# Turning keys and queries in fp32, in place and two head pairs at a time, with the instruction order drawn anew

## The chip, the cores and the metric

The kernel runs on one core of one Trainium2 chip. The metric is device time in microseconds (us): the median of several executions. The profile shows one further execution, taken by the hardware profiler. The engines are called as in the profile: PE is TensorE, DVE is VectorE, ACT is ScalarE, POOL is GpSimd, SP is SyncE, whose queue issues most of the DMAs.

## What is computed

Attention over selected chunks, and then a gated feed-forward layer. Cut from the reference:

```python
# q, k, v: 4 x 8 x 768 x 64 float32; chunks of 32 keys, 24 chunks; top_k = 6
k_min = np.min(k_chunks, axis=3); k_max = np.max(k_chunks, axis=3)
ub = sum(maximum(q * k_min, q * k_max), axis=-1)     # bound of each query on each chunk
ub = where(causal, ub, -1e9)
top_chunks = argsort(ub, axis=-1)[..., -6:]
scores = q @ k.T / 8
scores = where(selected and causal, scores, -1e9)
attn = softmax(scores)
x = (attn @ v), heads side by side                   # 3072 x 512
out = (sigmoid(x @ w_gate) * (x @ w_val)) @ w_out    # w_gate, w_val 512 x 1536; w_out 1536 x 512
```

## The kernel before

**Units.** The 3072 tokens are eight units, u0 to u7, of 384 tokens each. A unit goes through attention (bounds, choice, scores, exponential, mask, product with v) and then through the feed-forward layer. u0 to u2 hold the early tokens and turn their keys and queries on PE. Units u3 to u7 hold the later query blocks of batches 1 to 3 and turn keys and queries with DVE's 32 x 32 transposes; the change is about these.

**Keys of a batch** (`keys_blocks`, steps k, k16, kt, kx, hk, kcr). Four DMAs on SP (`load_blocks`, L660) bring the 768 keys of eight heads so that 32 x 32 blocks can be turned. For each of the four head pairs: the smallest and largest of every chunk straight from the raw fp32 tile by a DVE reduction that transposes as it reads (`extremes`, L684); a copy to f16 on POOL or ACT (k16, L459, L455); a DVE transpose of that copy (kt, L850); and two copies of it into the tiles that the scores read (hk, one for each head of the pair).

**Queries** (`turn_queries`, `queries_blocks`, `choose`). A DVE transpose per head pair takes the raw fp32 tile into a second tile qf (L866). From qf come the positive part qm (L698, L700) and the f16 copies hq. PE multiplies qf and qm with the chunk ranges in fp32 (ub, L899), the even and the odd heads each into a PSUM tile of their own. DVE transposes each (ubn, L910), bars unseen chunks (ubm), finds the largest eight of each row (mx, MAX8, L922), compares with the sixth (ap, L927) and transposes the result (apt, L933), again once for each of the two. Copies hqm put this mask beside the queries, so that the scores' matmul adds it.

**Attention's end** (`finish`). DVE divides by the row sums (rz L1012, x L1014). For u3 to u7 a transposing DMA on SP (L1019, step xT) turns x for the feed-forward layer.

**Feed-forward.** For u3 to u7 gate and value products (L1199) are made with seven products of half size in the place of eight: they need sums of weights (ss, L1170) and of tokens (tt, L1183), and steps that put the products together (e7, sd, c21, c22). The output projections of u4 to u7 are made in the same manner: sums of output weights (tw, L1052, twelve of them) and of hidden blocks (sw, L1082), products at L1092. The others are plain (o, L1321). DVE or POOL makes the sums.

**Order and room.** Every step is an operation with a cost per engine; a written list, ORDER, gives their sequence and each one's engine in 2097 entries (`kt_3_2=V` is the turning of batch 3's head pair 2 on DVE; P is PE, A ACT, V DVE, G POOL, S SP). Every engine, and SP's queue, works through its own part in that sequence. A second list, SLOTS, gives each buffer its place in one SBUF arena of 234 units, and each PSUM tile one of eight banks; a buffer may be written when the earlier holders of its place were last read. A third list, TIES, adds a few waits. Names end in unit or batch and part: x_u3_1 is x of unit 3, head pair 1.

Of the kernel before, what the change touches and what calls it, by code (L numbers as in the profile page):

```python
# [14 lines left out]
NEG = -60000.0  # L15
UNITS = 234
# [123 lines left out]
tanh_u1_6=A cm_u2_2=G v_u1_2=P hg_u1_9=V k11_2=S kcr_1=G osb_u0_2=A exp_u2_2_1=A sc_u2_1_2=P exp_u2_0_2=A exp_u2_3_1=A sc_u2_7_1=P  # L140
qf0_u3_1=V k10_2=S sc_u2_6_2=P pv_u2_4=P hq0_u3_0=G exp_u2_6_2=A hg_u1_7=V qf0_u3_2=V pv_u2_5=P v_u1_10=P v_u1_8=P exp_u2_7_1=A qf0_u3_3=V
qm_u3_0=A cm_u2_6=G exp_u2_1_2=A hg_u1_3=V v_u1_6=P hq1_u3_0=G hg_u1_2=V v_u1_11=P hg_u1_6=V hq1_u3_2=G hg_u1_11=V qm_u3_2=A ub_u3=P
hg_u1_8=V k01_2=S xpsf_3_0=P hq0_u3_2=G hk0_1_3=A ss3_g0=G o0_u1_1=P pv_u2_0=P ubn1_u3=V hk1_1_3=A ubn0_u3=V ubm1_u3=V xpsf_3_1=P
xTf_3_1=A kt_1_1=V mx1_u3=V hk1_1_2=A pv_u2_3=P hk0_1_1=A pv_u2_6=P xTf_3_0=A q00_2=S hg_u1_10=V qf0_u4_0=V pv_u2_2=P o1_u1_1=P v16_1_1=G
pv_u2_1=P pv_u2_7=P hk1_1_1=G ap1_u3=V rz_u2_2=V rz_u2_3=V apt1_u3=V rz_u2_0=V hk0_1_0=G x_u2_3=V rz_u2_1=V ubm0_u3=V o2_u1_1=P o0_u1_0=P
x_u2_2=V hk0_1_2=A o1_u1_0=P x_u2_0=V hqm1_u3_2=A q11_2=S osb_u1_1=A xps_u2_3=P sc_u3_7_1=P xT_u2_3=A exp_u3_7_1=A sc_u3_7_2=P mx0_u3=V
qf0_u4_2=V x_u2_1=V hqm1_u3_0=G sc_u3_4_0=P ap0_u3=V exp_u3_4_0=A v16_1_2=G kx1_2_1=V k16_2_3=G xps_u2_2=P apt0_u3=V xT_u2_2=A kx1_2_2=V
sc_u3_5_0=P exp_u3_7_2=A k16_2_0=G hqm0_u3_2=G q01_2=S o0_u1_2=P sc_u3_6_2=P sc_u3_4_2=P exp_u3_4_2=A sc_u3_6_1=P qf0_u4_1=V qf0_u4_3=V
exp_u3_5_0=A o1_u1_2=P k16_2_2=G exp_u3_6_2=A kx0_2_0=V hqm0_u3_0=G sc_u3_5_2=P kt_2_0=V exp_u3_5_2=A exp_u3_6_1=A xps_u2_1=P q10_2=S
sc_u3_6_0=P cm_u3_5=G sc_u3_4_1=P kt_2_3=V exp_u3_6_0=A cm_u3_6=G sc_u3_7_0=P xps_u2_0=P out_u0_1=S o2_u1_0=P xT_u2_1=A kx0_2_2=V  # L150
o2_u1_2=P kx1_2_3=V v_1_3=S xT_u2_0=A g_u2_2=P sc_u3_1_2=P v_1_4=S exp_u3_4_1=A sc_u3_0_1=P g_u2_11=P exp_u3_7_0=A cm_u3_4=G v_1_0=S
cm_u3_7=G sc_u3_5_1=P osb_u1_2=A exp_u3_1_2=A osb_u1_0=A kx0_2_3=V sc_u3_1_0=P k16_2_1=G hk0_2_3=G tanh_u2_11=A v_u2_0=P v_2_1=S
exp_u3_1_0=A cm_u3_1=G exp_u3_0_1=A exp_u3_5_1=A sc_u3_3_1=P qf1_u4_3=V sc_u3_1_1=P exp_u3_1_1=A exp_u3_3_1=A tanh_u2_2=A g_u2_8=P
hk1_2_0=G out_u1_0=S g_u2_10=P qf1_u4_2=V out_u1_1=S kx1_2_0=V qf1_u4_0=V k01_3=S k11_3=S sc_u3_0_2=P v_u2_10=P qf1_u4_1=V sc_u3_3_2=P
g_u2_9=P tanh_u2_10=A hq1_u4_2=G hg_u2_10=V kx0_2_1=V hq0_u4_2=G exp_u3_0_2=A tanh_u2_8=A g_u2_4=P sc_u3_2_1=P v_u2_8=P qf0_u5_1=V
qm_u4_2=A v16_1_3=G v_u2_9=P sc_u3_3_0=P exp_u3_3_2=A hq1_u4_0=G hg_u2_8=V kcr_2=G tanh_u2_9=A out_u0_2=S hg_u2_9=V sc_u3_0_0=P g_u2_0=P
exp_u3_2_1=A qm_u4_0=A g_u2_5=P v16_1_4=G exp_u3_0_0=A qf0_u5_2=V v16_1_0=G ub_u4=P cm_u3_0=G g_u2_3=P exp_u3_3_0=A hk1_2_3=G qf0_u5_3=V
pv_u3_6=P qf0_u5_0=V tanh_u2_0=A k10_3=S tanh_u2_4=A kt_2_1=V sc_u3_2_0=P v16_2_1=G qm_u5_0=A v_u2_11=P ubn0_u4=V tanh_u2_5=A qm_u5_2=A
ubn1_u4=V exp_u3_2_0=A hq1_u5_0=A hk0_2_1=G g_u2_7=P tanh_u2_3=A ubm0_u4=V out_u1_2=S pv_u3_0=P sc_u3_2_2=P exp_u3_2_2=A hg_u2_0=V
mx0_u4=V kt_2_2=V hq1_u5_2=A pv_u3_4=P pv_u3_1=P ap0_u4=V ubm1_u4=V tanh_u2_7=A hg_u2_11=V pv_u3_7=P apt0_u4=V g_u2_1=P v_1_5=S hq0_u4_0=G  # L160
hk1_2_1=G pv_u3_5=P g_u2_6=P tanh_u2_1=A mx1_u4=V k00_3=S hqm0_u4_2=A rz_u3_3=V v_u2_7=P cm_u3_3=G ub_u5=P hg_u2_7=V ap1_u4=V hk0_2_0=G
hk0_2_2=G tanh_u2_6=A x_u3_3=V sc_u4_2_0=P ubn1_u5=V sc_u4_2_2=P apt1_u4=V hqm0_u4_0=A v_u2_4=P v_u2_5=P rz_u3_2=V exp_u4_2_2=A
sc_u4_2_1=P rz_u3_0=V exp_u4_2_0=A sc_u4_1_1=P exp_u4_2_1=A hk1_2_2=G cm_u3_2=G v_u2_1=P hqm1_u4_2=G v_2_0=S ubn0_u5=V hqm1_u4_0=G
# [12 lines left out]
exp_u4_0_3=A pv_u4_0=P v_2_2=S sc_u5_5_0=P p6_g1_u3=P osb_u2_2=A sd_g0_u3=A p6_g0_u3=P p2_g0_u3=P sc_u4_5_2=P tanh_u3_100=A exp_u5_5_0=A
tanh_u3_000=A pv_u4_1=P x_u4_1=V cm_u4_5=G exp_u4_5_2=A p7_g2_u3=P e7_g2_u3=A p1_g2_u3=P tt3_u3=G c21_g1_u3=V p5_g1_u3=P c21_g0_u3=V
# [223 lines left out]
def kernel(  # L401
# [1065 lines left out]
```

## Time and profile before

| | |
|---|---|
| median of 3 runs | 274.91 us (274.8 to 275.87) |
| the profiled execution | 274.87 us |
| its span in the trace | 273.0 us |
| granted TensorE clock, mean | 0.994 |
| PE busy | 263.1 us, 3094 matmuls |
| DVE, ACT, POOL busy | 227.3, 208.6, 187.3 us |

The span runs from the first to the last instruction in the trace; 274.87 also holds what lies around it. Busy time is the time in which an engine executes something. PEld is PE's weight load, which lies beside its matmuls. In a row of a group stand the line, engine, operation, output and input, their shapes and the count, then the busy time of all and the mean ns of one, and last the idle time ahead of them with what ended it. A row of one line's instructions has the shortest, the median and the longest duration. A timeline row has start, duration, engine, line and operation, and in brackets the idle time before it and what ended that.

### The profile page before, as it was taken

The page shows a single profiled execution, that of the slowest core. Times are in us where ns is not written, and L with a number is a line of the kernel's source. Part 1 is how long each engine was busy: PE and PEld are TensorE (multiplying, and loading weights), DVE is VectorE, ACT ScalarE, POOL GpSimd, SP SyncE. Part 2 cuts the span into 40 slices and gives each one's busy share as a digit, 9 for nine tenths or more (in the row PEclk, how much of TensorE's full clock was granted, in tenths as well). Part 3 has the DMA queues.
Part 4 walks back from the last instruction along what each step waited for, and adds up shares of the span by engine and source line. Part 5 has one row for each costly group of instructions (what it writes and reads, how often), then busy time and mean ns, then how long its engine had stood idle before and what let it go on. Part 6 is the DMA issues. An engine that isn't in the chain of part 4 may idle for free.

```text
span 273.0 us, 8339 instructions
## 1 busy us (share of the span) xinstructions
PE 263.1 (96%) x3094; PEld 207.8 (76%) x3094; DVE 227.3 (83%) x654; ACT 208.6 (76%) x451; POOL 187.3 (69%) x287
## 2 busy tenths in 40 slices
PE   6979999999999999999999999999999999999994
PEld 4655658657666667675889878899988999999984
DVE  4789846788989989889989999889898879678861
ACT  6378878669886899899889999989998763665322
POOL 5796744658996799697499974887773556584440
PEclk9979999999999999999999999999999999999999
DMA  6999999999999999912783715130200020022035
GB/s 155 240 292 200 204 214 214 214 184 177 170 204 165 202 257 218 180 33 53 166 133 86 195 31 130 42 95 4 46 14 2 17 46 1 2 78 79 2 119 228
DMA packets 131576, 34.74 MB, mean 127 GB/s; under 512 B 119760, under 2 KB 128464, under 8 KB 131536
## 3 DMA queue, kind: packets, MB, share of 16 engines
q1 hardware_dynamic: 126768, 29.50, 50.8%
q0 software_dynamic: 4768, 4.72, 10.2%
q8 instruction: 24, 0.39, 0.6%
q14 instruction: 16, 0.13, 0.1%
HBM read 30.67 MB, written 6.29 MB: 135 GB/s over the span
## 4 chain that ended last, share of the span: by engine, by line
PE 85%; DVE 4%; DMA 4%; ACT 2%; issue 1%; POOL 1%; SPq 1%; DVEq 0%; ACTq 0%
PE sc_u L960 11%; PE g_u L1247 9%; PE o_u L1321 9%; PE v_u L1247 8%; PE pl_v_u L1199 7%; PE pv_u L993 6%; PE pl_g_u L1199 6%; PE pl_u L1092 6%; PE ps_v_u L1199 5%; PE ps_g_u L1199 4%; PE ps_u L1092 4%; PE ube_u L899 3%; DMA arena<-arena 3%; ACT arena L971 1%; DMA arena<-in_k_dram 1%
## 5 line engine op out<-in xcount | busy, mean ns | idle before, releaser
L971 ACT ACTIVATE arena<-sc_u 128x512 f16<-128x512 f32 (+3 forms) x184 | 90.4, 552 | 7.7 <-PE sc_u L960 6.3
L1082 POOL TENSOR_TENSOR arena<-arena 128x256 f16<-128x256 f16 x44 | 29.1, 682 | 23.6 <-DVE arena L1082 9.7
L977 POOL TENSOR_SCALAR_AFFINE_SELECT arena<-arena 128x384 f16<-128x384 f16 (+1 forms) x56 | 28.2, 515 | 18.5 <-DVE arena L1170 4.4
L1321 PE MATMUL o_u<-wo,arena 128*128 128x512 f16 x144 | 35.3, 379 | 0.0
L1199 PEld LDWEIGHTS <-arena 128*128 128x128 f16 x360 | 30.1, 98 | 1.9
L960 PE MATMUL sc_u<-hqe,hke 128*128 128x128 f16 (+2 forms) x220 | 28.9, 243 | 0.0
L1247 PE MATMUL g_u<-arena,wg 128*128 128x384 f16 x144 | 27.5, 326 | 0.9 <-ACT arena L455 0.6
L960 PE MATMUL sc_u<-hqo,hko 128*128 128x128 f16 (+2 forms) x220 | 28.3, 243 | 0.0
L1258 DVE SCALAR_TENSOR_TENSOR arena<-arena,v_u 128x384 f16<-128x384 f16 x36 | 19.2, 549 | 10.1 <-ACT arena L1254 5.6
L1247 PE MATMUL v_u<-arena,wv 128*128 128x384 f16 x144 | 27.2, 326 | 0.0
L993 PE MATMUL pv_u<-v,arena 128*128 128x65 f16 x640 | 26.3, 193 | 0.5 <-DVE arena L1014 0.5
L1092 PEld LDWEIGHTS <-arena 128*128 128x128 f16 x252 | 24.4, 98 | 2.4
L993 PEld LDWEIGHTS <-arena 128*128 128x128 f16 x640 | 24.3, 98 | 2.3 <-issue 0.6
L1321 PEld LDWEIGHTS <-arena 128*128 128x128 f16 x144 | 13.3, 98 | 11.1
L1199 PE MATMUL ps_g_u<-arena,wg 128*128 128x192 f16 x180 | 21.4, 246 | 0.3 <-DVE wg L1170 0.3
L1199 PE MATMUL ps_v_u<-arena,wv 128*128 128x192 f16 x180 | 21.6, 246 | 0.0
L1199 PE MATMUL pl_v_u<-arena 128*128 128x192 f16 x180 | 21.5, 246 | 0.0
L1199 PEld LDWEIGHTS <-wv 128*128 128x128 f16 x240 | 20.0, 98 | 1.8 <-issue 0.6
L1199 PEld LDWEIGHTS <-wg 128*128 128x128 f16 x240 | 20.1, 98 | 1.3 <-DVE wg L1170 0.4
L1199 PE MATMUL pl_g_u<-arena 128*128 128x192 f16 x180 | 21.0, 246 | 0.0
L1247 PEld LDWEIGHTS <-wg 128*128 128x128 f16 x144 | 13.4, 98 | 9.7 <-DMA wg<-in_moe_w_gate_dram 1.6
L1254 ACT ACTIVATE arena<-g_u 128x384 f16<-128x384 f32 x36 | 17.2, 497 | 4.2 <-PE g_u L1247 3.9
(159 smaller groups left out, 666.0 us busy)
## 6 DMA issues: line engine op xcount, KB each, us to landing
arena<-in_v_dram SPq DMA_DIRECT2D x27, 256.0 KB, 4.3
out_dram<-arena SPq DMA_DIRECT2D x24, 256.0 KB, 2.3
arena<-in_k_dram SPq DMA_DIRECT2D x12, 384.0 KB, 5.2
arena<-in_q_dram SPq DMA_DIRECT2D x12, 384.0 KB, 5.5
arena<-in_q_dram SPq DMA_DIRECT2D x12, 128.0 KB, 8.9
arena<-in_k_dram SPq DMA_DIRECT2D x12, 128.0 KB, 4.4
wv<-in_moe_w_val_dram POOLq DMA_DIRECT2D x3, 512.0 KB, 10.0
wo<-in_moe_w_out_dram POOLq DMA_DIRECT2D x3, 512.0 KB, 17.7
```

The lines of the kernel that those rows point to most:

```text
L899: nc.tensor.matmul(at(ub[e_])[32 * p:32 * p + 32, lo - u.s0:hi - u.s0], kcr[par][ROWS[e_], p, m, :], at(src)[ROWS[e_], p, lo:hi], start=(m ...
L960: nc.tensor.matmul(at(t)[:, o:o + 128 * m], hk[b % 2][e_][:, p, 128 * jb:128 * jb + 128], hq[u.side][e_][:, p, 128 * x:128 * (x + m)], sta ...
L971: plan.add(f"exp_{u.name}_{h}_{y}", {ACT: act(n)}, lambda e, t=t, att=att, b0=b0, n=n: nc.scalar.activation(at(att)[:, b0:b0 + n], at(t), ...
L977: nc.gpsimd.affine_select(out=dv, in_=dv, compare_op=ALU.is_ge, fill=0.0, base=0, pattern=[[0, u.m], [1, 128]], channel_multiplier=-1)
L993: nc.tensor.matmul(at(pv)[:, last, x, :], at(att)[:, c:c + 128], v16[b % 2][:, jb, h, :], start=(jb == 0), stop=(jb == ib))
L1082: plan.add(f"sw{n}_{name}_{j}", {DVE: dve(256, 2), POOL: pool2(256)}, lambda e, a=a, b=b, op=op, n=n, j=j: both(e).tensor_tensor(sums(n, j ...
L1092: nc.tensor.matmul(at(to), a(j)[:, i], b(j)[:, i], start=first and j == i == 0, stop=j == 2 and i == 1, skip_group_check=True)
L1199: nc.tensor.matmul(at(to)[:, s], a()[:, c, 128 * s:128 * s + 128], b()[:, c], start=first and s == c == 0, stop=c == 1, skip_group_check=True)
L1247: nc.tensor.matmul(at(t), w16[:, c, 128 * fb:128 * fb + 128], at(u.xt)[:, c, :], start=(c == 0), stop=(c == 3))
L1254: plan.add(f"tanh_{u.name}_{name}", {ACT: act(T, psum)}, lambda e: nc.scalar.activation(dst(), src(), AF.Tanh, scale=0.5), reads=reads, wr ...
L1258: plan.add(f"hg_{u.name}_{name}", {DVE: dve(T)}, lambda e: nc.vector.scalar_tensor_tensor(dst(), gate(), 1.0, src(), ALU.add, ALU.mult), r ...
L1321: nc.tensor.matmul(at(o), at(hgs[fc // 2])[:, fc % 2, 128 * tb:128 * tb + 128], wo16[:, fc, lo:hi], start=(fc == 0), stop=(fc == NFB - 1))
```

## The change

- **Keys.** Per two head pairs, one DVE transpose of 1536 elements turns the raw fp32 tile in place. Two plain reductions of 1536 read the turned tile, and the two hk copies of 1536 read it and cast to f16. The f16 copy k16 and the buffer of kt are gone. Per batch: 2 transposes, 4 reductions, 4 copies, where there were 4, 8, 4 casts and 8 copies.
- **Queries.** Turned in fp32 in place, two head pairs in one instruction. There is no qf for u3 to u7: qm, hq and the bounds' matmuls read the raw tile once it is turned, so its place in the arena is held until the bounds are made. qm and hq are split by the unit's segments.
- **Bounds.** For u3 to u7 both halves are in two adjacent PSUM banks, so ubn, ubm, ap and apt are one instruction each for the two. PSUM is one tile cut by slot.
- **Sums.** One of the four tw is written over a quarter of each block of output weights (after its last reader), and one of the four sw over the hidden block that it comes from; both buffers shrink from four to three. The sums of output weights are planned at the first unit that uses them. Twelve sw go from POOL to DVE, eight sums of 512 (ss, tw) from DVE to POOL.
- **Order.** ORDER (2023 entries), SLOTS and TIES are new. The first 431 entries are the same; the two differ from PE's next step after scf_3 on. The number of matmuls, their shapes and the DMAs on SP are unchanged. `MERGED` is empty, so the `wide` branches in `attend` do nothing.

Around the keys of batch 3, SP's order after is `v_2_0 q00_3 v_2_1 xT_u3_0 k01_3 xT_u3_2 out_u0_2 q11_3 xT_u3_1 k10_3 xT_u3_3 k00_3 k11_3`; before it was `k01_3 k11_3 out_u0_2 k10_3 out_u1_2 v_1_5 k00_3 v_2_0 q10_3 xT_u3_0 xT_u3_1`.

```diff
+MERGED = ()
...
+    bank = banks.tile([128, 8 * 512], F32, tag="bank", name="bank")
...
     def keys_blocks(b, raw, next_):
...
-        for p in range(NP):
-            extremes(par, f"{b}", p, lambda p=p: at(raw)[:, p], S, every, kx, slice(0, NC), blocks, True, next_)
-            k16 = Buf("np", f"k16_{b}_{p}", [128, NC, CH], F16)
-            kt = Buf("np", f"kt_{b}_{p}", [128, S], F16)
-            plan.add(f"k16_{b}_{p}", {POOL: pool(S), DVE: dve(S, 2), ACT: act(S, False)},
-                     lambda e, p=p, k16=k16: copy(e, at(k16), at(raw)[:, p]), reads=every, writes=[k16], port=True, prio=next_())
-            plan.add(f"kt_{b}_{p}", {DVE: dve(S)}, lambda e, k16=k16, kt=kt: nc.vector.transpose(
-                at(kt), at(k16).rearrange("p c d -> p (c d)")), reads=[k16], writes=[kt], prio=next_())
+        for p in range(0, NP, 2):
+            ps_ = (p, p + 1)
+            plan.add(f"kt_{b}_{p}", {DVE: dve(2 * S)}, lambda e, p=p: nc.vector.transpose(
+                flat(at(raw)[:, p:p + 2]), flat(at(raw)[:, p:p + 2])), reads=[(raw, i) for i in range(4)],
+                writes=[(raw, "turned", p)], prio=next_())
+            outs = [lambda p=p: kcr[par][:, p:p + 2, 0, 0:NC], lambda p=p: at(kx)[:, p:p + 2]]
+            for m, op in enumerate((ALU.min, ALU.max)):
+                plan.add(f"kx{m}_{b}_{p}", {DVE: dve(2 * S)}, lambda e, m=m, op=op, p=p, outs=outs: nc.vector.tensor_reduce(
+                    out=outs[m](), in_=at(raw)[:, p:p + 2], op=op, axis=AX.X), reads=[(raw, "turned", p)],
...
-                plan.add(f"hk{e_}_{b}_{p}", {POOL: pool(S), DVE: dve(S, 4, 64), ACT: act(S, False, 64)},
-                         lambda e, p=p, e_=e_, kt=kt: copy(e, hk[par][e_][ROWS[e_], p], at(kt)[ROWS[e_]]),
+                plan.add(f"hk{e_}_{b}_{p}", {POOL: pool(2 * S), DVE: dve(2 * S, 2, 64), ACT: act(2 * S, False, 64)},
+                         lambda e, p=p, e_=e_: copy(e, hk[par][e_][ROWS[e_], p:p + 2], flat(at(raw)[ROWS[e_], p:p + 2])),
...
     def turn_queries(u, seg, raw, next_):
...
-        for p in range(NP):
-            plan.add(f"qf{seg}_{u.name}_{p}", {DVE: dve(128 * m)}, lambda e, p=p: nc.vector.transpose(
-                at(u.qf)[:, p, 128 * x:128 * (x + m)], at(raw)[:, p, c0:c0 + 4 * m].rearrange("p c d -> p (c d)")),
+        u.raw = getattr(u, "raw", []) + [(raw, c0)]
+        for p in range(0, NP, 2):
+            def turn(e, p=p):
+                t = flat(at(raw)[:, p:p + 2, c0:c0 + 4 * m])
+                nc.vector.transpose(t, t)
...
     def queries_blocks(u, next_):
...
+        u.view = lambda s, p: flat(at(u.raw[s][0])[:, p:p + 1, u.raw[s][1]:u.raw[s][1] + 4 * u.segs[s][2]])[:, 0]
...
     def choose(u, next_):
-        ub = [ps(f"ub{'eo'[e]}_{u.name}", "ub", [128, u.n]) for e in range(2)]
+        both_ = u.i > 2
+        if both_:
+            ub = ps(f"ub_{u.name}", "ub", [128, 512 + u.n])
...
+                if both_:
+                    wide = bank[:, 512 * ub.slot:512 * ub.slot + 1024].rearrange("p (e n) -> p e n", e=2)[:, :, 0:u.n]
+                    nc.vector.transpose(at(ubn).rearrange("p e a c -> p e (a c)"), wide)
...
-    tw = Buf("tw", "tw", [128, 4, 3, 2, 256], F16)
+    tw = Buf("tw", "tw", [128, 3, 3, 2, 256], F16)
+    def t_out(n, j):
+        return wo16[:, 4 * j:4 * j + 2, 256:512] if n == 2 else at(tw)[:, n - (n > 2), j]
...
-        skey = Buf("sums", f"sums_{name}", [128, 3, 4, 2, 128], F16)
+        skey = Buf("sums", f"sums_{name}", [128, 3, 3, 2, 128], F16)
         def sums(n, j):
-            return at(skey)[:, j, n]
+            return block(j, 1, 0) if n == 2 else at(skey)[:, j, n - (n > 2)]
...
+        if u.i == PAIRED[0]:
+            weight_sums(base)
...
-    weight_sums(0.4)
```

## The prediction

> **What bounds the kernel now.** I read the busy times first, then the chain that ended last by engine.
>
> ```profile
> span 273.0 us, 8339 instructions
> PE 263.1 (96%) x3094; PEld 207.8 (76%) x3094; DVE 227.3 (83%) x654; ACT 208.6 (76%) x451; POOL 187.3 (69%) x287
> PE 85%; DVE 4%; DMA 4%; ACT 2%; issue 1%; POOL 1%; SPq 1%; DVEq 0%; ACTq 0%
> ```
>
> TensorE (PE) is busy 96% and carries 85% of the chain. An average over stages proves little, so next came the windows: width of the stretch, then each engine's busy time in it.
>
> ```profile
> core 0: us, PE busy (x) PEld busy (x) DVE busy (x) ACT busy (x) POOL busy (x), PEclk, DMA share, GB/s
> 57.00:110.00 53.00, 53.00 (x568) 34.49 (x565) 48.57 (x143) 46.13 (x98) 42.53 (x66) 1.00 1.08 194
> 110.00:130.00 20.00, 20.00 (x195) 12.70 (x194) 18.26 (x69) 18.12 (x38) 15.77 (x21) 1.00 0.49 92
> 130.00:150.00 20.00, 19.25 (x288) 17.69 (x287) 18.97 (x42) 18.16 (x41) 15.73 (x22) 1.00 0.65 128
> 150.00:200.00 50.00, 50.00 (x761) 44.27 (x759) 45.26 (x147) 46.33 (x95) 38.28 (x51) 1.00 0.30 74
> 200.00:260.00 60.00, 60.00 (x728) 55.87 (x726) 50.04 (x120) 37.16 (x88) 33.85 (x54) 1.00 0.09 28
> 260.00:273.00 13.00, 9.55 (x88) 8.31 (x85) 5.41 (x18) 3.42 (x10) 3.26 (x5) 1.00 0.47 181
> ```
>
> From 57 to 260 us PE is idle in one stretch only, 130 to 150, and there for 20.00 - 19.25 = 0.75 us, at the full granted clock. The engine that is nearly as full is VectorE (DVE): 18.97 of 20 us there, 18.26 of 20 in the stretch ahead. PE's timeline names both idle moments in brackets, and the chain shows what is behind them.
>
> ```profile
> 131.65 0.50 PE L1199 MATMUL ps_g_u<-arena,wg 128*128 128x192 f16 x4 [0.27 <-DVE wg L1170]
> 141.12 0.55 PE L993 MATMUL pv_u<-v,arena 128*128 128x65 f16 x13 [0.48 <-DVE arena L1014]
> ```
>
> ```profile
> 56.92 0.33 PE scf L749 x8
> 120.06 0.65 PE v_u L1247 x4
> 125.80 3.33 DMA arena<-arena
> 129.28 0.11 DVE arena L1183
> 130.29 1.30 DVE wg L1170
> 136.40 4.01 DMA arena<-arena
> 140.50 0.57 DVE arena L1014
> 269.58 0.38 ACT arena L1059
> ```
>
> Each begins with a transposing DMA of the attention output x. One takes 3.33 us; a token sum on DVE (L1183) needs it, and the weight sum (L1170) that PE waits for is queued behind it. The other takes 4.01 us and holds the room in which the next x (L1014) is written; PE's pv waits for that x's accumulator.
>
> **The frame of the sum.** The profiled execution took 274.87 us; its span is 273.0, so 1.87 us lie outside, and it stands 0.04 below the median of 274.91. The matrix products are the same in both kernels, number and shapes; the orders are the same up to PE's scf entry at 56.92 us. After it PE can win the 0.75 us. Matmul ends are modelled; measured between starts instead, the two delays are 1.1 us, the most I grant. The tail behind the last product (0.38 us at 269.58, output) is the same work: 0, at most 0.3 either way.
>
> **Keys and queries turned in fp32.**
>
> ```profile
> L850 DVE STREAM_TRANSPOSE arena<-arena 128x768 f16<-128x768 f16 x12 | 11.3, 951 | 0.0
> L684 DVE TRANSPOSE_TENSOR_REDUCE arena<-arena 128x24 f32<-128x768 f32 x12 | 11.2, 949 | 0.0
> L684 DVE TRANSPOSE_TENSOR_REDUCE kcr<-arena 128x24 f32<-128x768 f32 x12 | 11.2, 943 | 0.0
> L866 DVE STREAM_TRANSPOSE arena<-arena 128x384 f32<-128x384 f32 x12 | 6.1, 549 | 0.0
> L866 DVE STREAM_TRANSPOSE arena<-arena 128x128 f32<-128x128 f32 x8 | 2.1, 284 | 0.0
> L684 DVE TENSOR_REDUCE arena<-kT_u 128x12 f32<-128x384 f32 x4 | 2.2, 552 | 0.3 <-PE kT_u L798 0.3
> L684 DVE TENSOR_REDUCE kcr<-kT_u 128x8 f32<-128x256 f32 x4 | 1.6, 418 | 0.7 <-ACT arena L455 0.7
> L459 POOL CAST arena<-arena 128x768 f16<-128x768 f32 x11 | 9.0, 823 | 1.2 <-PE sc_u L960 0.7 <-DVE arena L1258 0.3
> L459 POOL COPY hke<-arena 64x768 f16<-64x768 f16 x9 | 7.3, 820 | 1.5 <-DVE ap L927 0.8 <-DVE arena L915 0.7
> L459 POOL COPY hke<-arena 64x1536 f16<-64x1536 f16 x1 | 1.5, 1457 | 0.1
> L1183 POOL TENSOR_TENSOR arena<-arena 128x384 f16<-128x384 f16 x11 | 10.0, 911 | 1.7 <-DVE arena L1258 0.9 <-DVE arena L1082 0.5 <-DVE arena L1012 0.2
> ```
>
> No row has a transpose or a plain reduce of 1536, so a line through the rows: transposes give (549 - 284)/256 = 1.035 ns per element and 152 ns to begin, hence 1.74 us; reduces (552 - 418)/128 = 1.047 and 150, hence 1.76. Keys: 36 instructions, 12 x (0.951 + 0.949 + 0.943) = 34.1 us, become 18 x 1.75 = 31.5: -2.6. Queries: 14 fewer transposes, each saving its 152 ns: -2.1. Bounds read as one pair: 15 fewer instructions at about 152 ns: -2.3. DVE loses 7.0 us. POOL loses 11 casts of 0.823 (-9.1). Its 16 key copies of 768 at 0.820 become 10 of 1536 at 1.457, 13.1 to 14.6 (+1.5); that they now read fp32 costs POOL nothing by its cast (823 against 820).
>
> The sums of the FFN change engines:
>
> ```profile
> L1082 POOL TENSOR_TENSOR arena<-arena x44: 664/668/1037, 203.0 to 265.7; 128x256 f16<-128x256 f16 x44
> L1082 DVE TENSOR_TENSOR arena<-arena x28: 251/284/752, 205.0 to 264.6; 128x256 f16<-128x256 f16 x28
> L1170 POOL TENSOR_TENSOR arena<-wv,arena x3: 1155/1156/1157, 72.0 to 144.0; 128x512 f16<-128x512 f16 x3
> L1052 DVE TENSOR_TENSOR arena<-wo,arena x5: 415/419/660, 203.8 to 223.4; 128x512 f16<-128x512 f16 x5
> ```
>
> Twelve of 256 go from POOL to DVE, 12 x 0.284 = +3.4 us; eight of 512 go the other way, -8 x 0.42 = -3.4; one token sum leaves POOL (0.91) and adds about 0.4 on DVE, an estimate from 0.284 for 256. DVE ends about 6.6 us lighter (3.5 if the long transposes and reduces run 7% over the line), POOL some 7 (-9.1 + 1.5 - 12 x 0.668 + 8 x 1.156 - 0.91 = -7.3). By the windows this lies wholly under a busy PE: 0 us of time, because PE is idle for 0.75 in all.
>
> The slowest of those DVE sums took 752 ns against a median of 284; at that price the twelve are 9.0 us instead of 3.4. The Trainium skill, "SBUF — State Buffer", section "Who interferes with whom", says that a VectorE instruction with two SBUF inputs contends with a GpSimd instruction that reads SBUF, which these sums are and would speak against moving them. DVE would still be about 1 us lighter, and from 200 to 260 us it has 10 us of air, so the sum stays.
>
> **What is moved in the order.** The old idle moments: after the change 11.6 us of PE's work lie between the last x of unit 3 and its first product, 6.5 before, by counting PE's entries at their present pace; against 3.33 us for the landing that stall goes. -0.75, at most -1.1. What is late next is unit 7: cover from x_u7_2 to the product that needs it shrinks from 11.8 to 6.2 us. And one thing waits that did not wait: the bounds now read the turned query tile, so its room comes free after ub_u4 and no longer after the turning. The keys of batch 3 (k3) are loaded into that room.
>
> ```profile
> L1019 SPq DMA_TRANSPOSE arena<-arena x20: 1177/1187/2235, 115.7 to 223.5; - x20
> DMA to landing us min/median/max: 2.3/2.4/4.4
> ...
> L660 SPq DMA_DIRECT2D arena<-in_k_dram x12: 383/1239/2927, 54.5 to 109.1; - x12
> DMA to landing us min/median/max: 3.8/5.4/6.4
> ...
> 123.97 0.96 DVE L684 TRANSPOSE_TENSOR_REDUCE kcr<-arena 128x24 f32<-128x768 f32 x1
> ```
>
> Before, the last was issued at 109.1 and they were first read at 123.97: over 8 us spare. After, three of the four stand on SyncE's (SP's) queue behind xT_u3_1, which waits for x_u3_1 on DVE. From x_u3_1 to kt_3_2, the first reader, the order has 111 matmuls: 59 of scores with 10368 columns, 24 of o (12288), 20 of v (7680), 8 products (1536), 31872 in all; at the chain's 0.65 us for 4 x 384 that is 0.423 ns per column, 13.5 us. In that time x_u3_1 (0.55), two transposing issues (1.19 each), two loads' issues (1.24 each) and the third load's landing (5.4) must pass: 10.8. That leaves 2.7 us. With the slowest issues (2.93 for the loads, 2.24 for the transposes) it is 10.8 + 2 x 1.69 + 2 x 1.05 = 16.3, or 17.3 with the slowest landing, 2.8 and 3.8 too late. DVE takes instructions in order: behind a waiting kt_3_2 are ss1_v0 and sd_g0_u3, and PE's second and sixth products of unit 3 wait for the latter, within some 2 us. Unit 7 similarly: two issues of 1.19, a landing of 2.4, a token sum on POOL of 0.91 are 5.7 of 6.2 us; with a landing of 4.4 it is 1.5 too late. I take 0.4 us of new idle for all of this (about half of the old 0.75, as the median rows leave spare in both places); bounds 0 and 2.5.
>
> Sum: 274.87 - 0.75 + 0.4 + 0 = 274.5 us.
>
> **Rivals.**
> *DVE is the real bound (faster).* If PE's busy matmuls hide waiting for DVE, the 6.6 us (3.5 to 7) of DVE work would show: 268.3 to 271.4, about 270. For it: DVE at 18.97 of 20. Against: where DVE is fullest PE waits 0.75 us. The Trainium skill, "Perfetto Trace Analysis", section "Identifying the Most-Contended Engine", has one judge TensorE by the busy time of its weight loads; these are 76%, and DVE with 83% would rank ahead. The trace disagrees: PE's starts follow one another without a gap from 57 to 131 us, where PEld is only 65% busy (34.49 of 53). Chance 0.06.
> *SP's queue is late (slower).* The k3 loads arrive after DVE reached kt_3_2. It decides once x_u3_1 and the issues behind it are over 2.7 us later than summed. Taken at 2.4 us, just under the 2.8 of all slowest issues: 274.5 + 2.4 = 276.9; DVE, full here, cannot catch up, so PE pays it whole. For it: those issue rows reach double their median when the queue is crowded. Against: between xT_u3_1 and the last of these loads only one other transfer stands on SP, so the chain is short. Chance 0.26.
> *The idle only moves.* New short waits of 0.75 to 2 us where the old were removed, at other x buffers and landings: 274.9 to 276.2. Chance 0.14.
> That the redrawn order is the old one in effect is excluded by the diff.
>
> **How the numbers follow.** The forecast (273.5 to 274.9) has 0.54. A measurement of this kernel can tell about 0.5%, 1.37 us, from no change: faster is under 273.54, slower over 276.28. Faster: the DVE rival's 0.06 and 0.02 of the forecast's lower end, 0.08. Slower: SP's 0.26. Same: 0.66. The range goes from 273.5 (274.87 - 1.1 - 0.3) to 276.9, where it leaves out the DVE rival and half of SP's case: 0.19.
>
> **What would show it.** Right: PE busy 96% with its windows from 57 to 260 full but for under 1 us; DVE about 219 to 222 us busy, POOL about 180; transposes and reduces of 1536 at 1.7 to 1.8 us with one line each; no L1170 sum and no x behind a transposing DMA on PE's chain. Wrong: idle PE behind a DVE transpose of the keys around 125 us with k loads landing just before it (SP rival); a span shorter by several us with the same matmuls (DVE rival); DVE's 256-sums near 0.75 us (contention).

## The result: slower by half a per cent, and the profile after

The changed kernel takes 276.44 us (median of 13 runs, 275.78 to 277.33) against 274.92 for the kernel before on the same chip: a ratio of 1.0047, 95% interval 1.0033 to 1.0061. In numbers it lies inside the range of the prediction, but the forecast was a small gain, and it is a small loss.

The page's head for the changed kernel:

```profile
span 275.0 us, 8236 instructions
PE 263.6 (96%) x3094; PEld 207.9 (76%) x3094; DVE 227.3 (83%) x608; ACT 204.6 (74%) x444; POOL 178.9 (65%) x262
```

Its windows, with the columns as before:

```profile
57.00:110.00 53.00, 53.00 (x602) 34.44 (x582) 47.31 (x107) 42.96 (x89) 43.33 (x60) 1.00 1.03 174
110.00:130.00 20.00, 20.00 (x193) 13.04 (x192) 18.85 (x79) 18.07 (x38) 12.50 (x15) 1.00 0.92 159
130.00:150.00 20.00, 20.00 (x291) 17.97 (x290) 18.59 (x30) 19.03 (x44) 17.43 (x24) 1.00 0.40 122
150.00:200.00 50.00, 50.00 (x760) 44.21 (x759) 44.04 (x134) 43.99 (x92) 34.48 (x50) 1.00 0.31 71
200.00:260.00 60.00, 58.27 (x707) 53.90 (x705) 51.73 (x121) 38.28 (x92) 30.86 (x41) 1.00 0.08 25
```

The idle 0.75 us of the stretch from 130 to 150 are gone: 20.00 of 20. They came back larger elsewhere: from 200 to 260 us PE is busy for 58.27 of 60, where it had been full. PE's own waits after 57 us (what it waited for, total, times, longest):

```profile
PE bank L1031 <- DVE arena L1302: 0.8, 1, 0.8
PE bank L1136 <- DVE arena L1126: 0.5, 1, 0.5
PE bank L992 <- DVE arena L1302: 0.4, 1, 0.4
```

Lines have moved: L1302 is the hidden product hg (before L1258), L1126 the hidden sums sw (L1082), L1096 the output-weight sums tw (L1052), L1227 the token sums tt (L1183), L1031 pv (L993), L992 scores (L960), L1136 the products of the output (L1092), L1243 the gate and value products (L1199), L1050 the reciprocal rz (L1012), L1159 the step that adds a product from PSUM onto an output (L1115). PSUM is one tile now and is called bank in every row. The chain of waits through the first of these places:

```profile
209.32 0.54 DVE arena L1302
209.86 0.86 DVE arena L1227 x2
210.72 0.07 DVE arena L1302
210.79 0.32 issue
211.11 1.30 DVE arena L1227
212.41 0.46 DVE arena L1302
212.88 0.10 DVE arena L1050
212.98 0.94 DVE arena L1227
213.93 0.48 DVE arena L1302
```

From 209.3 to 214.4 us the chain runs through DVE alone. Two token sums in it take 1.30 and (from 212.91) 1.02 us. Rows from the timelines of DVE and of POOL around these moments:

```profile
206.33 0.54 DVE L1302 SCALAR_TENSOR_TENSOR arena<-arena,bank 128x384 f16<-128x384 f16 x1
208.26 1.14 DVE L1302 SCALAR_TENSOR_TENSOR arena<-arena 128x384 f16<-128x384 f16 x1
211.11 1.30 DVE L1227 TENSOR_TENSOR arena<-arena 128x384 f16<-128x384 f16 x1
212.91 1.02 DVE L1227 TENSOR_TENSOR arena<-arena 128x384 f16<-128x384 f16 x1
```

```profile
205.47 1.16 POOL L1096 TENSOR_TENSOR arena<-wo,arena 128x512 f16<-128x512 f16 x1
207.83 1.15 POOL L1096 TENSOR_TENSOR arena<-wo,arena 128x512 f16<-128x512 f16 x1
210.81 1.40 POOL L1096 TENSOR_TENSOR arena<-wo,arena 128x512 f16<-128x512 f16 x1 [0.29 <-DVE arena L1227]
212.56 1.16 POOL L1096 TENSOR_TENSOR wo<-wo 128x512 f16<-128x512 f16 x1 [0.36 <-DVE arena L1227]
```

Each of the three long DVE instructions starts inside an output-weight sum on POOL, and ends 0.2 to 0.4 us after it: 209.40 after 208.98, 212.41 after 212.21, 213.93 after 213.72. These are three of the sums that the change moved from DVE to POOL (tw3_0, tw1_1, tw2_0). The hg at 206.33 also starts inside a POOL sum and takes its usual 0.54; it reads one input from SBUF (arena) and one from PSUM (bank). In the whole trace 19 hg of that kind start inside a POOL sum, and they take 0.51 to 0.56 us, like the others.

The second place is the wait of 0.54 us at 257.88, for a hidden sum on DVE:

```profile
253.08 1.31 DVE L1126 TENSOR_TENSOR arena<-arena 128x256 f16<-128x256 f16 x2
254.90 2.40 DVE L1126 TENSOR_TENSOR arena<-arena 128x256 f16<-128x256 f16 x5
258.08 1.08 DVE L1126 TENSOR_TENSOR arena<-arena 128x256 f16<-128x256 f16 x5
```

```profile
251.33 2.92 POOL L1126 TENSOR_TENSOR arena<-arena 128x256 f16<-128x256 f16 x4 [0.60 <-PE bank L1243]
254.47 1.59 POOL L1126 TENSOR_TENSOR arena<-arena 128x256 f16<-128x256 f16 x2 [0.23 <-DVE arena L1126]
256.36 0.79 POOL L1126 TENSOR_TENSOR arena<-arena 128x256 f16<-128x256 f16 x1 [0.29 <-DVE arena L1126]
```

Five sums on DVE take 2.40 us while POOL sums as well (three of them 0.64 to 0.75 us each), and five take 1.08 us once POOL is done.

Measured between starts, as in the prediction, the two places cost PE 0.93 + 0.58 and 0.71 us, 2.2 in all; the two old ones, 1.1, are gone. That is 1.1 us net of the 2.0 between the two spans. Another 0.8 came earlier, in the part that is the same in both kernels: on the chain PE's scf entry, the last common one, begins at 57.72 us here and at 56.92 before. This part varies from one execution to the next, so it is better left out: from the first matmul of scf_3 (57.65 us here, 56.85 before, by PE's timelines) to the end of the span the changed kernel takes 217.4 us and the kernel before 216.1, and a second profile of the changed kernel, with a span of 274.3, gives 217.4 again. By this measure, called "after scf" below, the change costs 1.2 us; the medians differ by 1.5 us.

### The profile page after: what moved, and what is told of

Its sections match the earlier page's. It is cut to its first block, busy times and chain, and to the rows that moved or that the text cites. A ratio compares the mean times of both kernels' runs of the same rounds, so it can differ in the third digit from the quotient of the medians.

```text
span 275.0 us, 8236 instructions
## 1 busy us (share of the span) xinstructions
PE 263.6 (96%) x3094; PEld 207.9 (76%) x3094; DVE 227.3 (83%) x608; ACT 204.6 (74%) x444; POOL 178.9 (65%) x262
## 4 chain that ended last, share of the span: by engine, by line
PE 79%; DVE 7%; DMA 5%; POOL 5%; issue 2%; ACT 0%; POOLq 0%
PE bank L1243 25%; PE bank L1291 13%; PE bank L992 12%; PE bank L1367 11%; PE bank L1136 8%; PE bank L1031 6%; DMA wg<-in_moe_w_gate_dram 5%; PE bank L913 3%; DVE arena L1302 2%; DVE arena L1126 1%; DVE arena L1227 1%; POOL arena L747 1%; PE bank L789 1%; DVE arena L448 1%; POOL hke L450 1%
## 5 line engine op out<-in xcount | busy, mean ns | idle before, releaser
L1009 ACT ACTIVATE arena<-bank 128x512 f16<-128x512 f32 (+3 forms) x184 | 89.8, 553 | 11.0 <-PE bank L992 10.0
L1302 DVE SCALAR_TENSOR_TENSOR arena<-arena,bank 128x384 f16<-128x384 f16 x81 | 42.8, 547 | 14.1 <-ACT arena L1298 5.6
L1298 ACT ACTIVATE arena<-bank 128x384 f16<-128x384 f32 x81 | 38.4, 495 | 11.6 <-PE bank L1291 5.1
L1243 PE MATMUL bank<-arena 128*128 128x192 f16 x360 | 41.5, 246 | 0.0
L1126 POOL TENSOR_TENSOR arena<-arena 128x256 f16<-128x256 f16 x32 | 22.0, 701 | 22.1 <-DVE arena L1126 14.4
L1367 PE MATMUL bank<-wo,arena 128*128 128x512 f16 x144 | 36.1, 379 | 0.0
L1243 PEld LDWEIGHTS <-arena 128*128 128x128 f16 x360 | 30.2, 98 | 1.0
L992 PE MATMUL bank<-hqo,hko 128*128 128x128 f16 (+2 forms) x220 | 29.7, 243 | 0.4 <-DVE arena L1302 0.4
L1291 PE MATMUL bank<-arena,wg 128*128 128x384 f16 x144 | 27.6, 326 | 1.8 <-DMA wg<-in_moe_w_gate_dram 1.2
L1243 PE MATMUL bank<-arena,wv 128*128 128x192 f16 x240 | 28.1, 246 | 0.0
L992 PE MATMUL bank<-hqe,hke 128*128 128x128 f16 (+2 forms) x220 | 28.1, 243 | 0.0
L1291 PE MATMUL bank<-arena,wv 128*128 128x384 f16 x144 | 27.7, 326 | 0.0
L1243 PE MATMUL bank<-arena,wg 128*128 128x192 f16 x240 | 27.0, 246 | 0.0
L1136 PEld LDWEIGHTS <-arena 128*128 128x128 f16 x252 | 24.4, 98 | 3.4 <-DVE arena L1126 0.8
L1031 PE MATMUL bank<-v,arena 128*128 128x65 f16 x640 | 26.1, 193 | 0.8 <-DVE arena L1302 0.8
L1031 PEld LDWEIGHTS <-arena 128*128 128x128 f16 x640 | 24.1, 97 | 2.8 <-issue 0.9
L992 PEld LDWEIGHTS <-hko 128*128 128x128 f16 x220 | 17.2, 98 | 5.5 <-issue 0.9
L1243 PEld LDWEIGHTS <-wg 128*128 128x128 f16 x240 | 20.3, 98 | 1.3
L1243 PEld LDWEIGHTS <-wv 128*128 128x128 f16 x240 | 20.0, 98 | 1.6 <-issue 0.6
```

The lines of the kernel that those rows point to most:

```text
L992: nc.tensor.matmul(at(t)[:, o:o + 128 * m], hk[b % 2][e_][:, p, 128 * jb:128 * jb + 128], hq[u.side][e_][:, p, 128 * x:128 * (x + m)], sta ...
L1009: plan.add(f"exp_{u.name}_{h}_{ys[0]}", {ACT: act(n)}, lambda e, t=t, att=att, b0=b0, n=n: nc.scalar.activation(at(att)[:, b0:b0 + n], at( ...
L1031: nc.tensor.matmul(at(pv)[:, last, x, :], at(att)[:, c:c + 128], v16[b % 2][:, jb, h, :], start=(jb == 0), stop=(jb == ib))
L1126: plan.add(f"sw{n}_{name}_{j}", {DVE: dve(256, 2), POOL: pool2(256)}, lambda e, a=a, b=b, op=op, n=n, j=j: both(e).tensor_tensor(sums(n, j ...
L1136: nc.tensor.matmul(at(to), a(j)[:, i], b(j)[:, i], start=first and j == i == 0, stop=j == 2 and i == 1, skip_group_check=True)
L1243: nc.tensor.matmul(at(to)[:, s], a()[:, c, 128 * s:128 * s + 128], b()[:, c], start=first and s == c == 0, stop=c == 1, skip_group_check=True)
```

## The experiments

Two theories stood against each other. A: DVE instructions with both inputs in SBUF are held up while POOL reads SBUF. B: DVE simply has too much work queued at these places. The runs below were made on three chips, where the kernel before takes 274.92 us (the first four runs), 275.86 (the next four) and 275.47 (the last three); so each time is compared with the kernel before on its own chip, and each profile, by the time after scf, with the changed kernel's 217.4 us. PE's starts after scf move against the changed kernel's only at the waits named, to within 0.1 us.

**Three output-weight sums on DVE.** In the changed kernel's order:

```diff
-tw3_0=G  tw1_1=G  tw2_0=G
+tw3_0=V  tw1_1=V  tw2_0=V
```

> The changed kernel with three output-weight sums of 512 (tw3_0, tw1_1, tw2_0) given from POOL to DVE, at the same places of the order. In the changed kernel they run on POOL from 207.83 to 213.71 us, and three DVE instructions beside them take 1.14, 1.30 and 1.02 us where the same forms take 0.54, 0.35 and 0.35 alone; PE then waits 0.77 + 0.42 us for DVE. Theory A (contention: DVE instructions with two SBUF inputs are held up while POOL reads SBUF): DVE gains 3 x 0.42 = 1.25 us of work and loses 2.2 us of holding up, so the waits at 213 and 214.5 us shrink or go; 0.6 to 1.5 us faster than the changed kernel, 274.9 to 275.8. Rival B (DVE simply has too much work queued at this place): 1.25 us more of it, so the waits grow to 2.0 to 2.5 us; 276.8 to 277.7.

275.40 us; ratio to before 1.0019 (1.0003 to 1.0035), against 1.0047; after scf 1.1 us less. DVE has three sums more, and PE waits less: of the three waits only that at the second place is left, at its 0.5 us. Two short ones are new between starts, 0.19 and 0.22 us, some 10 us later.

The two theories had opposite signs, and A's came.

**The same three on POOL, without reading.**

```diff
-                made.append(plan.add(..., lambda e, ...: both(e).tensor_tensor(
+                made.append(plan.add(..., lambda e, ...: nc.gpsimd.memset(out_(n), 0.0) if (n, j) in ((3, 0), (1, 1), (2, 0)) else both(e).tensor_tensor(
```

> The changed kernel in which the same three sums stay on POOL at their places but only fill their output with zeros, so POOL reads nothing from SBUF for them (the sum is left out; the output projections of units 4 to 7 then use zeros there). DVE's work and order are untouched. Theory A (contention by POOL's reading): the three DVE instructions return to 0.35 to 0.55 us, the waits of PE at 213 and 214.5 us go, about 1.2 to 1.6 us faster than the changed kernel, 274.8 to 275.3. Rival B (DVE's queue): the waits stay, 276.2 to 276.7.

274.88 us; ratio 0.9997 (0.9974 to 1.0021); after scf 1.5 us less, which is the two waits at the first place and nothing else. The token sums, shortest, median and longest, here and in the changed kernel:

```profile
L1227 DVE TENSOR_TENSOR arena<-arena x10: 309/352/360, 127.0 to 229.5; 128x384 f16<-128x384 f16 x10
```

```profile
L1227 DVE TENSOR_TENSOR arena<-arena x10: 308/352/1301, 126.5 to 230.5; 128x384 f16<-128x384 f16 x10
```

DVE's order and work were as in the changed kernel; POOL's reading was gone, and with it the waits. POOL's work became shorter too (0.52 us for 1.15), but that is not the reason: two token sums still start inside a zero fill (at 211.00 in the one from 210.62 to 211.14, at 211.84 in the one from 211.47 to 212.00) and take 0.34 and 0.31 us. B, by which the waits should have stayed, falls for this place.

**Seven hidden sums on DVE.** sw0_u7_0, sw0_u67_0, sw2_u7_0, sw3_u5_1, sw2_u67_2, sw2_u67_0 and sw1_u67_2 from G to V.

> The changed kernel with the seven sums of 256 that POOL runs from 251.33 to 257.15 us given to DVE at the same places of the order. Five of DVE's own sums take 0.64 to 0.75 us there against 0.28 elsewhere, and PE waits 0.54 us at 257.88. Theory A: the five return to 0.28 (with overlapping starts 0.2 apart), DVE gains 7 x 0.2 to 0.28 = 1.4 to 2.0 and loses about 2.2 us, so the wait goes or stays as it is: 0 to 0.7 us faster, 275.7 to 276.4. Rival B: 1.4 to 2.0 us more in DVE's queue just ahead of the wait: 277.5 to 278.4.

277.02 us; ratio 1.0085 (1.0056 to 1.0114); after scf 0.9 us more: slower, as B had it, though by less than B's figure, and not for B's reason. DVE's sums were short again, six in 1.30 and seven in 1.49 us by its timeline:

```profile
253.53 1.30 DVE L1126 TENSOR_TENSOR arena<-arena 128x256 f16<-128x256 f16 x6
255.37 0.42 DVE L1159 SCALAR_TENSOR_TENSOR arena<-bank,arena 128x256 f32<-128x256 f32 x1 [0.54 <-PE bank L1136]
255.71 0.48 DVE L1126 TENSOR_TENSOR arena<-arena 128x256 f16<-128x256 f16 x2
256.39 0.42 DVE L1159 SCALAR_TENSOR_TENSOR arena<-bank,arena 128x256 f32<-128x256 f32 x1 [0.20 <-PE bank L1136]
256.74 1.49 DVE L1126 TENSOR_TENSOR arena<-arena 128x256 f16<-128x256 f16 x7
```

```profile
PE bank L1136 <- DVE arena L1126: 1.3, 2, 0.7
```

By PE's starts the old wait is gone (0.70 us less at the product that had it), and two new ones have come at other products: 0.91 us just ahead of it (at 257.07 here) and 0.72 us at 261.31. DVE was not full there: by the rows above it stood idle for 0.54 and 0.20 us until PE had made what L1159 reads, and the sum that PE then waited for at 257.07 came behind that step in DVE's order. So this mend removes the contention but puts sums behind steps that themselves wait for PE. By these traces it is the order, and not the amount of DVE's work, that cost here; no run changes the order alone to prove it.

**All ten on DVE.**

> The changed kernel with all ten of these sums on DVE. Theory A: the gains add up, 0.8 to 2.0 us faster than the changed kernel, 274.4 to 275.6, about level with the kernel before. Rival B: 2.6 to 3.2 us slower than the changed kernel.

276.11 us; ratio 1.0040 (1.0013 to 1.0067); after scf 0.2 us less. The first place is mended, the second made worse; the two edits add up (-1.1 and +0.9), and both theories' figures missed that.

**The seven on POOL, without reading.**

```diff
-                plan.add(f"sw{n}_{name}_{j}", ..., lambda e, ...: both(e).tensor_tensor(
+                plan.add(f"sw{n}_{name}_{j}", ..., lambda e, ...: nc.gpsimd.memset(sums(n, j), 0.0) if f"{n}_{name}_{j}" in (
+                    "0_u7_0", "0_u67_0", "2_u7_0", "3_u5_1", "2_u67_2", "2_u67_0", "1_u67_2") else both(e).tensor_tensor(
```

> The changed kernel in which the seven hidden sums that POOL runs from 251.33 to 257.15 us stay on POOL but only fill their output with zeros (the sums are left out; products of units 5, 6 and 7 read zeros there). DVE's work and order are as in the changed kernel. With seven sums more on DVE the wait of PE at 257.88 had grown from 0.71 to 0.88 and a second of 0.73 had come, so here DVE's queue is the path. Theory A (contention adds to that queue): DVE's five sums of 0.64 to 0.75 return to 0.28, the wait at 257.88 goes, 0.5 to 0.8 us faster than the changed kernel. Rival B (only the amount of DVE's work counts): the wait stays at 0.7.

275.81 us; ratio 0.9990 (0.9965 to 1.0014). The wait at the second place is gone; those at the first stand (line numbers are one higher in this file):

```profile
PE bank L1031 <- DVE arena L1303: 0.8, 1, 0.8
PE bank L992 <- DVE arena L1303: 0.4, 1, 0.4
```

After scf it is 0.7 us less, just the wait at the second place, and inside A's 0.5 to 0.8. The ratio is lower than 0.7 us would make it, and even its upper end is; the changed kernel did not run on this chip, which gave the kernel before 275.86, so why is open. With DVE's work untouched, POOL's reading decides this place too: the DVE sums take 0.28 to 0.29 us, those that start inside a zero fill as well.

**Three hidden sums earlier.** sw1_u5_2 and sw3_u45_2 move from 253.64 and 255.46 us to behind the sum at 247.82, and sw3_u5_1 moves up on POOL.

```diff
-... sw1_u5_2=V ... sw3_u45_2=V        (among the sums of unit 7)
+sw2_u6_1=V sw1_u5_2=V sw3_u45_2=V
+sw1_u6_1=G sw3_u5_1=G                 (its tie to hg_u7_211 left out)
```

> The changed kernel with three hidden sums that are ready earlier moved up in the order: sw1_u5_2 and sw3_u45_2 from among the sums of unit 7 on DVE (253.64 and 255.46, 0.75 each there) to behind sw2_u6_1 (247.82), and sw3_u5_1 on POOL to behind sw1_u6_1, without its tie. Theory A: they cost 0.28 each where POOL's sums are fewer, DVE's chain ahead of the wait at 257.88 loses up to 1.5 us, and the 0.71 us there go: 275.7 to 276.0 against 276.44. Rival: what waits for them, or the products ahead, was not set by DVE's chain, and the wait stays: 276.2 to 276.7.

276.03 us; ratio 0.9996 (0.9971 to 1.0021); after scf 0.5 us less, and the ratio is again lower than that makes it. The wait at 257.9 is gone, the two at 213 and 214.5 stand; between starts one of 0.19 at 250.1 is new.

**Both mends.**

> Both mends: three output-weight sums on DVE (which gave 275.4) and the three hidden sums moved up. Theory A: 1.0 + 0.7 us off the changed kernel, 274.5 to 275.0, level with the kernel before. If it ends at 275.4 or over, the second place was not mended.

275.28 us; ratio 0.9970 (0.9943 to 0.9997). The time is over the 274.5 to 275.0 expected, on a chip that gave the kernel before 275.86; after scf it is 1.7 us less, the 1.0 + 0.7 expected. None of the three waits is left, only three of 0.2 us between starts. After scf this kernel takes 215.7 us, 0.4 less than the kernel before.

**Output-weight sums on POOL, on the kernel before.** This is close to one part of the change, but not the same: the change moves seven of these eight (tw2_2 stays on DVE) and brings three others to DVE.

```diff
-tw0_0=V tw1_1=V tw3_1=V tw1_0=V tw2_0=V tw2_2=V tw3_0=V tw3_2=V
+tw0_0=G tw1_1=G tw3_1=G tw1_0=G tw2_0=G tw2_2=G tw3_0=G tw3_2=G
```

> One part of the change alone, on the kernel before: the eight output-weight sums that DVE makes from 202.78 to 223.83 us are given to POOL at the same places of the order; all else is as before. DVE loses 8 x 0.42 = 3.4 us of work. If DVE's work were what counts, the time stays or falls (274.4 to 275.0). Theory A (contention): token sums and hidden sums of DVE from 204.97 to 216.22 us, at 0.28 to 0.35 beside an idle POOL, now meet POOL's reading and take 0.7 to 1.3; new waits of PE between 205 and 222 us, 0.3 to 1.5 us slower, 275.2 to 276.4.

277.10 us; ratio 1.0044 (1.0014 to 1.0075); after scf 1.5 us more than the kernel before, 1.1 of it at the product below and 0.4 behind the last product. DVE has eight sums, 3.4 us, less to do and the kernel is slower (DVE's busy time stays at 227.1). DVE, POOL and PE there:

```profile
202.11 2.65 DVE L1258 SCALAR_TENSOR_TENSOR arena<-arena 128x384 f16<-128x384 f16 x2
```

```profile
204.31 1.46 POOL L1052 TENSOR_TENSOR arena<-wo 128x512 f16<-128x512 f16 x1
```

```profile
205.28 0.59 PE L1321 MATMUL o_u<-wo,arena 128*128 128x512 f16 x2 [0.92 <-DVE arena L1258]
```

POOL makes four sums in one piece from 199.2 to 204.3 and a fifth behind them. Two hg with both inputs in SBUF take 2.65 us beside that, where the form takes about 0.55 each, and PE waits for the second. A's sign came, but its victims were to be token and hidden sums; the wait came from hg. In the kernel before, POOL's output-weight sums end by 200.4, and from 203 to 213 us POOL is busy for only 4.1 of 10 us (8.0 in the changed kernel).

**The changed kernel and the mended ones on one chip.** The last adds two sums to a hole of 1.14 us that DVE has at 204.8:

```diff
+hg_u5_200=V tw1_1=V tw3_1=V          (their ties to tt0_u6 and hg_u5_101 left out)
-... tw1_1=V ... tw3_1=G ...
```

> The changed kernel once more, beside the mended ones on one chip and against the same runs of the kernel before: 0.3 to 0.6% slower than before; PE's waits at 213, 214.5 and 257.9 us as in its first profile (0.77, 0.42, 0.54).

> The kernel with both mends again (three output-weight sums on DVE, three hidden sums moved up). Theory A: the three waits stay away; 0.3 to 0.8% faster than the changed kernel here, and 0 to 0.4% faster than the kernel before, since its two old waits (0.75 us) are gone as well. Rival: the waits of the changed kernel were chance of one execution, and the two kernels come out alike.

> Both mends, and two of the output-weight sums (tw1_1 from its place near 219.6 us on DVE, tw3_1 from POOL at 220.1) moved to a hole of 1.14 us that DVE has at 204.8, without their ties. Theory A: DVE is less pressed at 219 to 222 us and POOL reads less there, so the remaining short waits of PE at 222.3 and 224.8 (0.19 and 0.23 between starts) shrink: 0 to 0.4 us faster than with both mends. If tw sums at 204.8 push the chain there, a new wait appears between 205 and 212 us and it is slower by up to 0.5.

276.66, 275.43 and 274.64 us, against 275.47 for the kernel before: ratios 1.0053 (1.0023 to 1.0082), 1.0002 (0.9975 to 1.0029) and 0.9961 (0.9930 to 0.9993). The three waits were in the second profile of the changed kernel with the same sizes (0.8, 0.5, 0.4), so they are no chance. With both mends the kernel is level with the one before here, and ahead of it by 0.3% on the other chip: level or a little better; after scf it takes 215.7 us again. With the two sums in the hole it is the fastest of all, by the medians 0.7% under the changed kernel and 0.3% under the one before; after scf it takes 215.3 us, 0.4 less than with both mends, which is what was expected at most, and the two waits of 0.2 near 222 and 225 us are gone. The medians' 0.8 between these two is more than that. The windows of this last kernel (width, PE, PEld, DVE, ACT, POOL):

```profile
57.00:200.00 143.00, 143.00 (x1838) 109.63 (x1823) 128.88 (x347) 124.06 (x260) 108.12 (x147) 1.00 0.67 129
200.00:260.00 60.00, 59.97 (x726) 55.75 (x724) 53.42 (x132) 39.05 (x94) 26.56 (x37) 1.00 0.09 25
```

PE is full from 57 to 260 us, with DVE more loaded (53.42) and POOL less (26.56) than in the changed kernel (51.73 and 30.86).

## Why the prediction was wrong, point by point

**What bounds the kernel: right.** PE did, and the loss is PE's waiting. The DVE rival is not borne out. The changed kernel alone is no test of it, as DVE's busy time did not fall; but with three zero fills on POOL it fell to 224.9 us, and PE gained its two waits and nothing elsewhere.

**The turning in fp32: the rows right, the saving too large.** The rows of 1536 came out at the line drawn through the smaller ones (1.74 and 1.76):

```profile
L840 DVE STREAM_TRANSPOSE arena<-arena 128x1536 f32<-128x1536 f32 x6 | 10.5, 1758 | 0.0
L845 DVE TENSOR_REDUCE arena<-arena 128x48 f32<-128x1536 f32 x6 | 10.3, 1739 | 0.0
L845 DVE TENSOR_REDUCE kcr<-arena 128x48 f32<-128x1536 f32 x6 | 10.2, 1724 | 0.0
```

The forecast took whole durations off DVE, 7.0 us for keys, queries and bounds. Neighbouring DVE instructions overlap in the trace (seven sums of 0.28 us end within 1.49), so an instruction fewer frees less: counted by what each adds behind the end of the one before it, the three together fell by 3.7 us. Nothing of PE's time hung on it, as was said: the last mended kernel keeps all of it, and PE is full there.

**The old idle moments: right.** No x and no weight sum waits behind a transposing DMA in PE's way; 20.00 of 20. With the contention mended, the kernel takes 0.4 us less after scf than the kernel before, and 0.8 less with the hole used too: about the small gain that was forecast.

**SP's queue (the slower rival, 0.26): not what happened.** Its cause was there: the transposing DMA xT_u3_1 took 3.58 us to issue for the 1.19 summed (the longest in the row of its line), xT_u3_3 took 2.32, and the last k3 load was issued only at 122.27. That load, by the DMA issues from 122.25 to 122.6 us, took 5.5 us to land, as summed (5.4), and DVE's timeline has the first reader:

```profile
L1057 SPq DMA_TRANSPOSE arena<-arena x20: 1177/1227/3582, 109.1 to 223.2; - x20
```

```profile
arena<-in_k_dram SPq DMA_DIRECT2D x1, 384.0 KB, 5.5
```

```profile
128.37 1.77 DVE L840 STREAM_TRANSPOSE arena<-arena 128x1536 f32<-128x1536 f32 x1
```

That is about 127.8, and kt_3_2 began at 128.37, right behind the instruction before it: 0.6 us to spare of the 2.7 worked out. The slow issues took the rest; in the profile of the last mended kernel some 0.2 us are left. So this rival failed narrowly. Unit 7 did not wait either. The 0.4 us of new idle were put at these two places; they cost nothing.

**The idle only moves (0.14): the form, not the cause.** New short waits did come, of 0.4 to 0.8 us. But they stand at hidden products and hidden sums and not at x buffers and landings, and the time, 276.44, is over this rival's 276.2.

**The sums: the step that failed.** "By the windows this lies wholly under a busy PE: 0 us." It measured 2.2 us of new waiting; with the two old waits gone, 1.2 us net. Three things were wrong in it. First, only the twelve sums moved *to* DVE were priced for contention. The eight moved *to POOL* went in as relief, 3.4 us off DVE, though three of them make the waits at the first place: token sums and hg, which stay on DVE, met them. The twelve and the eight are also net counts: by ORDER 26 hidden sums go to DVE and 14 to POOL, and of the seven on POOL at the second place six were on DVE before. Second, the price was set against an average, "10 us of air" in 60. DVE had that air still (51.73 busy of 60), but in order and elsewhere: what counts is whether a POOL sum lies beside a DVE sum within a few us of a product that needs it. Third, the price used, 752 ns against a median of 284, is that of a meeting with a POOL sum of 256 and no upper bound: a DVE sum waits for the rest of POOL's instruction and ends 0.2 to 0.4 us later, so the bound is set by the POOL instruction, 1.16 us for a sum of 512 by itself. The token sum of 1.30 is that, beside a POOL sum that was itself drawn out to 1.40. At the second place the price named came true, as the prediction's last sign of being wrong had it: five sums of 0.64 to 0.75 us.

So "DVE about 219 to 222 us busy" failed as well: 227.3, just as before. The mean of the token sums on DVE rose from 354 ns (nine of them) to 540 (ten), and that of the hidden sums from 306 (28) to 334 (40):

```profile
L1227 DVE TENSOR_TENSOR arena<-arena 128x384 f16<-128x384 f16 x10 | 5.3, 540 | 0.0
L1126 DVE TENSOR_TENSOR arena<-arena 128x256 f16<-128x256 f16 x40 | 12.0, 334 | 0.2
```

Against 352 and 282 ns when alone the excess is 10 x 0.19 + 40 x 0.05 = 4 us of DVE time. Counted again by what each instruction adds behind the one before it, all these sums together take 2.2 us more than before and not the 0.4 forecast; the other 1.5 us of the missing relief of 3.7 are spread over other steps and not explained here. POOL, at 178.9 us, came out as forecast (about 180).

The Trainium skill, "SBUF — State Buffer", section "Who interferes with whom", which the prediction cited and set aside, says more than was used: it calls the port pair that VectorE and GpSimd share an exclusive lock, has issue order decide who blocks, and says that a GpSimd instruction that only writes SBUF does not contend with a VectorE instruction of two SBUF inputs. The traces agree: in the changed kernel's, all eleven DVE instructions with two SBUF inputs that start inside a POOL sum end 0.15 to 0.42 us after it, and beside zero fills the sums take 0.28 to 0.34. The eight sums on POOL could have been a rival of their own, with up to 1.16 us at each meeting.

**What stays open.** Of the medians' 1.5 us, 1.2 are placed in the profiles after scf. The rest is within what the common first part varies between executions: scf_3 began between 56.3 and 58.3 us in the profiles of the changed kernel and of its variants. What makes that part vary was not looked into.

## What to carry to other kernels

Before moving elementwise sums from one of VectorE and GpSimd to the other, list what each of them runs at that moment: work moved *off* VectorE can slow VectorE, if it goes to GpSimd beside instructions with two SBUF inputs. Where such sums must be shared, put them on GpSimd where VectorE works from PSUM, or on VectorE in a hole of its own, and not behind a VectorE step that waits for TensorE. Air in an average over 60 us hides nothing for an engine that works in order: look at the 5 us ahead of the product that needs the sum.

## What the runs showed of the hardware that was not expected

A VectorE instruction of two SBUF inputs that started inside a GpSimd sum ended 0.15 to 0.42 us after it, in all eleven such cases of the changed kernel's trace, however short it is by itself: 1.30 us for 0.35, 1.14 for 0.55. GpSimd pays as well, 1.40 us for 1.16. On VectorE alone, seven sums of 256 ran in 1.49 us (in the run with seven hidden sums on DVE), while five of them took 2.40 beside GpSimd's three: at that moment the eight sums took longer on two engines than seven on VectorE alone, though where the sums stand in the order still decided the kernel's time. And a transposing DMA's issue, 1.23 us at the median, took up to 3.58 us on SP's queue; a query load and an output store issued just ahead of it were still in flight.
